# Linear attention into a GELU feed-forward: w_in in two pieces behind the third unit's logits, full-width inter products, seven state buffers, pair results in two stores

## The chip, the cores and the metric

One core of a Trainium2 chip runs the whole kernel. The metric is device microseconds of one execution, and lower is better. The core has TensorE (PE, matmuls; its weight loads are shown as PEld), VectorE (DVE), ScalarE (ACT), GpSimd (POOL) and SyncE (SP, which here only issues transfers). Every engine works through its own list of instructions strictly in order; engines wait for each other through semaphores, and transfers run on 16 DMA engines that all queues share.

## What is computed

Four batches, eight heads, 768 tokens, head size 48. First a gated linear attention with a running state, then a feed-forward block with exact GELU on the 3072 tokens of 384 values:

```python
f = 1.0 / (1.0 + np.exp(-f_logit))
for t in range(S):
    state = f[:, :, t, :, None] * state + np.einsum('bhd,bhe->bhde', k[:, :, t], v[:, :, t])
    y[:, :, t] = np.einsum('bhd,bhde->bhe', q[:, :, t], state)
x = y.transpose(0, 2, 1, 3).reshape(B * S, H * D)      # 3072 x 384
h = x @ w_in                                           # 384 x 2048
g = 0.5 * h * (1.0 + erf(h / sqrt(2)))
out = g @ w_out                                        # 2048 x 384
```

Inputs and output are float32; the matmuls of the kernel run in bf16.

## The kernel before

The tokens are cut into 24 chunks of 128 (six per batch). Two chunks make a *unit* (0 to 11); a unit is also one *group* of the feed-forward. The kernel does not emit instructions where it describes them: `Plan.add` collects operations with an engine, an assumed duration, a priority and their buffers, `Plan.run` places them one after another by earliest start and then priority (jittered by the random seeds in `SEEDS`), and the last loop emits them in that order. So each engine's list is the planner's order, and on the chip nothing overtakes in it. Buffers come from `Slots`; the eight PSUM banks `ps` are split into four for the feed-forward (`s_fh`) and four for attention (`s_m`, also `s_ap`). Where the planner left TensorE idle in the first 30 us, the emitting loop fills in matmuls on a zero tile (`junk`, L947).

Operations are named in the plan; these names, with the unit or chunk number behind them, are used in what follows:

- **E, L** (ACT, L494, L497): exp and log of one minus the gate, on the unit's loaded logits `fl`. **C** (PE, L521 or L526/L527, with the column sums L515/L523): running sums of the logs. **G** (DVE, L535): in the units of `G1D` the second chunk's sums are not multiplied again but are the first's minus one term. **RG, GT, GL** (ACT, L543, L549, L565/L570): exponentials of the sums.
- **KP, QP** (DVE, some POOL, L576): scaled k and q, into `sc`. **VC** (POOL or ACT, L583): v in bf16.
- **Tk, Tq** (PE, L611): transposes of `sc`; **KQ** (DVE or ACT, L617) copies them to `kq`. In units 4 to 11 (`KDMA`) a DMA transpose **KD** (SP, L599) does both.
- **A** (PE, L784 in pair units, L722 in others): scores; **AM** (DVE, L631): masking.
- **S** (PE, L806/L745): k times v of a chunk; **R** (DVE, L651/L655), **T** (POOL, L657) and **SB** (POOL, L662) carry the state from chunk to chunk.
- **YI** (PE, L826) and **YX** (PE, L705): output inside the chunk, and from the carried state; **Y** (L758, L699) is both in units that are no pair. **YB** (L675) evacuates; **XT** (PE, L691) and **X** (L694), or a DMA transpose **XD** (L679), give `xT`.
- **F1.g.u** (PE, L875): six 128x256 matmuls, tile u of group g of x w_in; tiles 0 to 3 need the first 1024 columns of w_in, 4 to 7 the rest. **GE** (ACT, L885): GELU. **F2.n.r** (PE, L896): quarter r of g w_out for chunk n, which needs tiles 2r and 2r+1. **O** (L901) evacuates, **st** (SP, L906) stores.

exp/log and GELU live in different ACT tables: each change costs a table load (L953).

Units 0 to 4 are *pair* units (`PAIRS`): a partition holds two neighbouring tokens, so that one descriptor brings 96 values, and matmuls use half or a quarter of the array (`mode=1` in the plan). GELU puts the tokens of these units back in order by a strided write.

Loads are issued in the order of `LOADS`: f, k, v, q of a unit by SP, pieces of w_in (`i`) and w_out (`o`) by POOL, as instructions in POOL's list (`ii`, `io`). When the issuing queue changes, the transfer waits for an earlier one of the other queue to land (the "gate" in `load`): a POOL load waits for the one four places back, an SP load for one two places back. So `i0` (1024 columns) waits for the landing of f1, and `i1` for that of k2:

```python
LOADS = ['f0', 'k0', 'v0', 'q0', 'f1', 'v1', 'k1', 'q1', 'i0', 'k2', 'f2', 'v2', 'q2', 'i1', 'i2', 'i3', 'o0', 'o1', 'o3', 'o2', 'f3', ...]
```

Of the kernel before, what the change touches and what calls it, by code (L numbers as in the profile page):

```python
# [15 lines left out]

# [7 lines left out]
TURN = 0.1  # L24

SPREAD, SEED = (1.0, 97)

SEEDS = [1643, 41, 3215, 1275, 2533, 2502, 823, 887, 1264, 763, 2447, 3095]

NUDGE = {}  # L30
XA = 0.0
# [48 lines left out]
class Op:  # L80
    __slots__ = ("eng", "dur", "fn", "bufs", "prio", "deps", "table", "start", "end", "vis", "seq", "name",
                 "left", "outs", "inst", "chain", "opens", "lag", "lat", "port", "mode", "held")


class Plan:

# [3 lines left out]
    def add(self, eng, dur, fn, rd=(), wr=(), bufs=(), prio=0.0, deps=(), table=None, name="", chain=None, opens=None, lag=0.0, lat=None, port=False, mode=0, held=False):  # L92
# [5 lines left out]
        o.held = held  # L98
        o.seq = len(self.ops)
# [16 lines left out]
    def run(self):  # L116
        free = dict.fromkeys(list(LAT), 0.7)
        free["DMA"] = 1.8
        rng = random.Random(SEED)
        own = [random.Random(x) for x in SEEDS]  # L120
        for o in self.ops:
            if o.prio > -5:
                k = min(max(int(o.prio % 1000) // 20, 0), len(SEEDS) - 1)
                o.prio += rng.uniform(-SPREAD, SPREAD)
                if SEEDS[k]:
                    w = (0.5, 1.0, 3.0, 8.0)[SEEDS[k] % 4]
                    o.prio += own[k].uniform(-w, w)
            o.prio += NUDGE.get(o.name, 0.0) + (XA if o.table == "exp" and o.prio > 40 else 0.0)
# [10 lines left out]
        while ready:  # L139
# [28 lines left out]
            if o.eng == "PE" and o.mode != mode:  # L168
                mode = o.mode
                d += TURN  # L170
# [29 lines left out]

SIZES = [2, 2, 2, 2, 2, 2, 2, 2, 2, 2, 2, 2]
PAIRS = [0, 1, 2, 3, 4]
WIN = [1024, 512, 512]
EG = [0, 1]
ET = [0, 1]
EX = [0]
EA = [0]
SPLIT = []  # L220
HVC = [1]
HKQ = [0, 2, 6]
HYB = [1, 5]
HX = [4]
GKP, GQP = ([2], [3])
GAM = []
ODVE = [0, 1, 2, 4, 6, 7, 8, 9, 10, 11, 12, 13, 14, 16, 17, 18, 19, 20, 21, 22, 23]
XDMA = [5, 6, 7, 8, 9, 10, 11]
KDMA = [4, 5, 6, 7, 8, 9, 10, 11]
AJ = [2, 3, 4, 5, 6, 7, 8, 10, 11]  # L230
NGT = 4
GLD = []
G1D = [2, 3, 4]
YJ = [2, 3, 4]
ROWS = [16, 17, 18, 19]
AMX = []
WARM = 30.0
LOADS = ['f0', 'k0', 'v0', 'q0', 'f1', 'v1', 'k1', 'q1', 'i0', 'k2', 'f2', 'v2', 'q2', 'i1', 'i2', 'i3', 'o0', 'o1', 'o3', 'o2', 'f3', 'k3', 'q3', 'u4', 'v3']
LOADS += [f"u{n}" for n in range(12) if f"u{n}" not in LOADS and f"c{2 * n}" not in LOADS and f"f{n}" not in LOADS]
# [3 lines left out]
def kernel(  # L243
# [14 lines left out]
    NCH = B * nC  # L258
    d_model = moe_w_in.shape[0]
# [42 lines left out]
    s_rr, s_tn = slots(3, [C, P2, 2 * D], F32, "rr"), slots(3, [C, P2, 2 * D], F32, "tn")  # L302
    s_sb = slots(3, [C, P2, 2 * D], BF16, "sb")
    s_yb = slots(3, [C, 2, HD], BF16, "yb")
    s_os = slots(4, [C, d_model], F32, "osb")
    s_xT = {s: slots({1: 4, 2: 4}.get(s, 2), [C, s, KO, C], BF16, f"xT{s}") for s in set(SIZES)}
    s_gT = {s: slots({1: 4, 2: NGT}.get(s, 2), [C, FO, s * C], BF16, f"gT{s}") for s in set(SIZES)}
# [15 lines left out]

# [30 lines left out]
    for i in range(3):  # L354
        P.add("DVE", 0.2, lambda i=i: nc.vector.memset(
            s_sb.tiles[i].rearrange("p a b -> p (a b)").bitcast(F32), 0.0), wr=[f"sbz{i}"], prio=-70)
# [5 lines left out]
    z_sb = [f"sbz{i}" for i in range(3)]  # L362
# [7 lines left out]
    U = [dict(fl=s_fl.new(), lf=s_lf.new(), pair=u in PAIRS, **{nm: s_in[nm].new() for nm in s_in}) for u in range(NU)]  # L370
# [8 lines left out]

    order, pools = [], []  # L380

    def load(eng, issue, wr, bufs, dur, name):
        i = len(order)
        gate = None
        if i and order[i - 1][0] != eng:
            back = 4 if eng == "pool" else 2
            for j in range(i - back, -1, -1):
                if order[j][0] != eng:
                    gate = order[j][1]
                    break  # L390

# [9 lines left out]
        if prev is not None and order[-1][0] != eng:  # L401
            prev.lat = 2.2
        gd = [gate] if gate is not None else []
        if eng == "pool":
# [15 lines left out]
    def src(a, n):  # L420
        b, c = divmod(n, nC)
        return a[b, :, c * C:(c + 1) * C, :].rearrange("h t d -> t h d")

    def srcp(a, u):
        b, c = divmod(2 * u, nC)
        return a[b, :, c * C:(c + 2) * C, :].rearrange("h (p j) d -> p h (j d)", j=2)

    win_src = moe_w_in.rearrange("(kk p) f -> p kk f", p=C)
    wo_src = moe_w_out.rearrange("(r p j) m -> r p j m", r=4, j=4)
    for what in LOADS:  # L430
        m = int(what[1:])
        if what[0] in "ucfkqv":
# [5 lines left out]
            if x["pair"]:  # L438
                assert what[0] != "c"
                for nm, a in names:  # L440
                    if what[0] not in ("u", nm[0]):
                        continue
                    if nm == "fl" and m in SPLIT:
                        for i in range(2):
                            load("sp", lambda x=x, a=a, m=m, i=i: nc.sync.dma_start(
                                out=x["fl"].t().rearrange("p (h x) -> p h x", h=H)[:, 4 * i:4 * i + 4], in_=srcp(a, m)[:, 4 * i:4 * i + 4]),
                                [("fl", 2 * m + i)], [x[nm]], 0.85, f"fl{m}.{i}")
# [12 lines left out]
        elif what[0] == "i" and m < len(WIN):  # L460
            load("pool", lambda m=m: nc.gpsimd.dma_start(out=win[m], in_=win_src[:, :, wcol[m]:wcol[m] + WIN[m]]),
                 [f"win{m}"], [], {512: 1.97, 1024: 3.95}[WIN[m]] + (0.5 if order[-1][0] == "sp" else 0.0), what)
# [4 lines left out]
    def decays(u):  # L467
# [33 lines left out]
        last = 2 * u + 1 if (2 * u + 1) % nC == nC - 1 else None  # L501
# [84 lines left out]

    St = {}

# [3 lines left out]
    def turn(u, kq):  # L592


        for j in range(2):
# [13 lines left out]
            def trans(i, tpv=tpv, sc=sc):  # L609
# [7 lines left out]
            P.add("ACT" if help_ else "DVE", 0.86 if help_ else 0.61, lambda tpv=tpv, j=j, help_=help_: copier(help_)(  # L617
                kq.t()[:, :, :, j, :].rearrange("a i p t -> a (i p) t"), tpv().rearrange("a i p t -> a (i p) t")),
# [17 lines left out]
    def carry(n, sp, mm, mmdur, mmrd, mmbufs, first_c):  # L636
# [16 lines left out]
        else:  # L653
            old = St["t"]
            P.add("DVE", 0.475, lambda: nc.vector.tensor_tensor(rr.t(), spf(), old.t(), ALU.add),  # L655
                  rd=[("sp", n), ("tn", n - 1)], wr=[("rr", n)], bufs=[sp, rr, old], prio=pr + PRI["S"] - 0.5, name=f"R{n}")
            P.add("POOL", 0.83, lambda: nc.gpsimd.tensor_tensor(tn.t(), rr.t(), glb(), ALU.mult),  # L657
                  rd=[("rr", n), ("gl", n)], wr=[("tn", n)], bufs=[rr, tn, gl], prio=pr + 2, name=f"T{n}")
        St["t"] = tn
# [42 lines left out]
    def interp(yp, kq, cc, osb):  # L702
        for p in range(P2):
            for j in range(2):
# [3 lines left out]
    def attn_nat(u):  # L708
# [3 lines left out]
        for j in range(2):  # L712
# [11 lines left out]
            if u in AJ:  # L724
                both.append((n, amm, aps, ams))
                if j:
                    P.add("PE", 0.46, lambda both=tuple(both): [b[1]() for b in both], mode=1, rd=[("kq", n - 1), ("kq", n)],
# [5 lines left out]
            P.add("PE", 0.23, amm, mode=1, rd=[("kq", n)], wr=[("ap", n)], bufs=[kq] + aps + ams, prio=pr + PRI["A"], opens=aps[0], name=f"A{n}")  # L733
            mask_scores(aps, ams, ("am", n), f"AM{n}", ("ap", n), pr, mask, "mask")
        for j in range(2):
            n = 2 * u + j
            c, x, pr = n % nC, X[n], 10 * n
            sc, vb, ams = x["sc"], x["vb"], amss[j]
            osb = St.get("sb") if c else None
            if c < nC - 1:  # L740
# [6 lines left out]
                St["sb"] = carry(n, sp, smm, 0.175, [("kp", n), ("vb", n)], [sc, vb], c == 0)  # L747
# [4 lines left out]
            def ymm(j=j, ams=ams, vb=vb, yp=yp, osb=osb):  # L752
                if osb is not None:
                    inter(yp, lambda p: kq.t()[:, 1, p, j, :], osb, True)
                for hh in range(2):
# [6 lines left out]
                  rd=[("am", n, 0), ("am", n, 1), ("vb", n), ("kq", n)] + ([("sb", n - 1, 0), ("sb", n - 1, 1)] if c else []),  # L762
# [3 lines left out]
    def attn_pair(u):  # L766
# [6 lines left out]
        sps = [s_m.new(), s_m.new()] if (n0 + 1) % nC < nC - 1 else [s_m.new()]  # L773
        ams, both = [], []
        for jk in range(2):
# [3 lines left out]
            def amm(jk=jk, aps=aps):  # L779
                for p in range(P2):  # L780
                    for cc in range(2):
                        for hh in range(2):
                            r, t = slice(64 * hh, 64 * hh + 64), slice(64 * cc, 64 * cc + 64)
                            nc.tensor.matmul(aps[hh].t()[t, p * C:(p + 1) * C].rearrange("a (j t) -> a j t", j=2),  # L784
# [16 lines left out]
        def smm():  # L801
            for p in range(P2):
# [6 lines left out]
        P.add("PE", 0.45, smm, mode=1, rd=[("kp", n) for n in ns] + [("vb", n) for n in ns],  # L809
              wr=[("sp", n) for n in ns[:len(sps)]], bufs=sps + scs + vbs, prio=pr + PRI["S"], opens=sps[0], name=f"S{u}")  # L810
        osb = St.get("sb") if n0 % nC else None
        for cc in range(len(sps)):
            St["sb"] = carry(ns[cc], sps[cc], None, 0, None, None, ns[cc] % nC == 0)
            if not cc:
                mid = St["sb"]
# [16 lines left out]
        if u in YJ:  # L832
            olds = [(cc, o) for cc, o in enumerate((osb, mid)) if o is not None]

            def joint():
                intra()
                for cc, o in olds:
                    interp(yps[cc], kq, cc, o)
            P.add("PE", 0.5 + 0.2 * len(olds), joint, mode=1,
# [147 lines left out]
```

## Time and profile before

| | |
|---|---|
| Median of 3 runs | 182.56 us (182.15 to 182.91) |
| Span of the profiled execution, first to last instruction | 181.1 us |
| Granted TensorE clock | 1.00 |
| TensorE busy | 171.7 us, 95% of the span |
| ACT, DVE, POOL busy | 125.2, 96.3, 53.6 us |
| First F1 matmul starts | 20.67 us |
| F1 matmuls (576) and F2 matmuls (368 of 384 columns) | 68.7 and 66.0 us busy |
| ACT table loads | 15, of 1.28 us |

The profiled execution's own time is not listed apart from its span; the median of the runs lies 1.5 us above the span, and that is taken for what lies around it (launch, and the end of the last store). "Busy" counts a matmul from its first to its modelled last cycle, so consecutive matmuls overlap: a 128x256 matmul is shown 273 ns long, but the next starts 109 ns after it. A wait is therefore read from the start of one instruction to the start of the next, and not from the busy share alone.

### The profile page before, as it was taken

The numbers are of one execution on the slowest core, as the hardware profiler recorded it, in microseconds if no ns is written. First come the engines' busy times: TensorE is split into PE (matmuls) and PEld (weight loads), VectorE is DVE, ScalarE is ACT, GpSimd is POOL, SyncE is SP. The second block draws the span as 40 slices with busy tenths as digits, with TensorE's granted clock in tenths as the row PEclk, the third lists the DMA queues.
The fourth block names the chain that finished last, engine by engine and source line by source line (L and its number), as shares of the span: only waits on it lengthen the run. The fifth ranks groups of instructions, "written<-read, shape, count | busy, mean of one in ns | idle before, by whom it ended". The sixth has DMA issues, their size and how long they took to land.

```text
span 181.1 us, 4916 instructions
## 1 busy us (share of the span) xinstructions
PE 171.7 (95%) x1990; PEld 132.3 (73%) x1990; DVE 96.3 (53%) x194; ACT 125.2 (69%) x212; POOL 53.6 (30%) x116
## 2 busy tenths in 40 slices
PE   7788889999999999988999999999999999999993
PEld 2356669966787688785779689976697986886972
DVE  5289750058898564244896692527691625362110
ACT  2775198963899189999967759777585578560720
POOL 7657870003043641140176113112435110300000
PEclk9999999999999999999999999999999999999999
DMA  6999999949997898999999999999999872814102
GB/s 148 261 261 226 268 170 203 200 115 267 278 266 142 186 197 170 249 227 171 216 179 213 215 175 207 195 187 189 185 245 181 181 162 47 166 37 91 43 0 87
DMA packets 106998, 32.61 MB, mean 180 GB/s; under 512 B 102113, under 2 KB 106081, under 8 KB 106977
## 3 DMA queue, kind: packets, MB, share of 16 engines
q1 hardware_dynamic: 105056, 29.07, 79.7%
q0 software_dynamic: 1776, 3.15, 9.8%
q8 instruction: 15, 0.25, 0.6%
q10 hardware_dynamic: 144, 0.10, 0.2%
q14 instruction: 7, 0.05, 0.1%
HBM read 25.17 MB, written 4.72 MB: 165 GB/s over the span
## 4 chain that ended last, share of the span: by engine, by line
PE 64%; ACT 15%; DMA 15%; SPq 3%; issue 1%; DVE 0%; DVEq 0%
PE ps L875 26%; PE ps L896 25%; ACT gT L885 7%; DMA fl<-in_f_logit_dram 7%; DMA win<-in_moe_w_in_dram 5%; ACT L953 4%; SPq L449 3%; DMA kq<-sc 2%; PE ps L722 2%; PE ps L758 2%; PE ps L917 1%; ACT gt L549 1%; PE ps L521 1%; PE ps L699 1%; PE ps L745 1%
## 5 line engine op out<-in xcount | busy, mean ns | idle before, releaser
L885 ACT ACTIVATE gT<-ps 128x512 bf16<-128x512 f32 x96 | 57.5, 671 | 24.6 <-PE ps L875 23.0
L875 PE MATMUL ps<-xT,win 128*128 128x256 bf16 x576 | 68.7, 273 | 1.3 <-ACT gT L885 0.9
L896 PE MATMUL ps<-wout,gT 128*128 128x384 bf16 x368 | 66.0, 326 | 0.0
L875 PEld LDWEIGHTS <-win 128*128 128x128 bf16 x576 | 61.6, 114 | 3.9 <-issue 1.2
L896 PEld LDWEIGHTS <-gT 128*128 128x128 bf16 x368 | 34.2, 98 | 19.5
L583 POOL CAST vb<-vt 128x384 bf16<-128x384 f32 x22 | 12.6, 584 | 52.5 <-DMA vt<-in_v_dram 52.4
L631 DVE TENSOR_TENSOR am<-ps,mask 128x512 bf16<-128x512 f32 x28 | 17.6, 684 | 15.1 <-PE ps L722 15.1
L901 DVE COPY osb<-ps 128x384 f32<-128x384 f32 x20 | 11.1, 556 | 25.9 <-PE ps L896 18.2
L657 POOL TENSOR_TENSOR tn<-rr,gl 128x384 f32<-128x384 f32 x16 | 14.0, 872 | 35.2 <-DVE rr L655 34.6
L576 DVE TENSOR_TENSOR sc<-qt,gt 128x384 bf16<-128x384 f32 x23 | 14.0, 616 | 13.7 <-ACT gt L549 13.7
L576 DVE TENSOR_TENSOR sc<-kt,rg 128x384 bf16<-128x384 f32 x23 | 13.5, 597 | 11.3 <-ACT rg L543 11.3
L953 ACT ACT_TABLE_LOAD x15 | 19.2, 1283 | 0.3
L662 POOL CAST sb<-tn 48x192 bf16<-48x192 f32 x40 | 14.8, 371 | 11.6 <-DVE tn L651 6.6
L494 ACT ACTIVATE fl<-fl 128x768 f32<-128x768 f32 x12 | 10.1, 842 | 10.5 <-DMA fl<-in_f_logit_dram 10.5
L675 DVE CAST yb<-ps 128x384 bf16<-128x384 f32 x22 | 11.9, 555 | 7.4 <-PE ps L758 3.7
L631 DVE TENSOR_TENSOR am<-ps,maskp 128x512 bf16<-128x512 f32 x20 | 12.5, 684 | 2.2 <-PE ps L784 1.4
L543 ACT ACTIVATE rg<-ps 128x384 f32<-128x384 f32 x21 | 10.3, 503 | 4.4 <-PE ps L523 2.8
L549 ACT ACTIVATE gt<-ps 128x384 f32<-128x384 f32 x21 | 10.2, 503 | 3.9 <-PE ps L523 3.3
L947 PE MATMUL ps<-junk 128*128 128x512 bf16 (+3 forms) x36 | 10.4, 423 | 2.1 <-POOL junk L939 1.3
L655 DVE TENSOR_TENSOR rr<-ps,tn 128x384 f32<-128x384 f32 x16 | 8.9, 553 | 3.5 <-POOL tn L657 1.8
L497 ACT ACTIVATE lf<-fl 128x768 bf16<-128x768 f32 x12 | 10.1, 843 | 0.4
L947 PEld LDWEIGHTS <-junk 128*128 128x128 bf16 x36 | 3.6, 111 | 6.2 <-issue 3.5
(74 smaller groups left out, 130.4 us busy)
## 6 DMA issues: line engine op xcount, KB each, us to landing
out_dram<-osb SPq DMA_DIRECT2D x19, 192.0 KB, 3.1
fl<-in_f_logit_dram SPq DMA_DIRECT2D x14, 192.0 KB, 3.8
kt<-in_k_dram SPq DMA_DIRECT2D x14, 192.0 KB, 3.8
qt<-in_q_dram SPq DMA_DIRECT2D x14, 192.0 KB, 3.7
vt<-in_v_dram SPq DMA_DIRECT2D x14, 192.0 KB, 3.9
fl<-in_f_logit_dram SPq DMA_DIRECT2D x5, 384.0 KB, 6.2
kt<-in_k_dram SPq DMA_DIRECT2D x5, 384.0 KB, 6.2
vt<-in_v_dram SPq DMA_DIRECT2D x5, 384.0 KB, 5.7
```

What stands on the lines that cost most here:

```text
L549: P.add("ACT", 0.40, lambda g=gps[j], gtv=gtv: nc.scalar.activation(gtv(), g.t()[:, 0:HD].rearrange("q (p h d) -> q p h d", h=2, d=D), AF. ...
L576: P.add("POOL" if pl else "DVE", 0.80 if pl else 0.475, lambda a=a, y=y, j=j, w=w, pl=pl, b=(gtv if w else rg): (nc.gpsimd if pl else nc.v ...
L583: P.add("ACT" if hv else "POOL", 0.40 if hv else 0.47, lambda y=y, j=j, hv=hv: (nc.scalar.copy if hv else nc.gpsimd.tensor_copy)(y["vb"].t ...
L631: P.add("POOL" if pl else "DVE", 1.15 if pl else 0.61, lambda hh=hh, pl=pl: (nc.gpsimd if pl else nc.vector).tensor_tensor(ams[hh].t(), ap ...
L657: P.add("POOL", 0.83, lambda: nc.gpsimd.tensor_tensor(tn.t(), rr.t(), glb(), ALU.mult), rd=[("rr", n), ("gl", n)], wr=[("tn", n)], bufs=[r ...
L662: P.add("POOL", 0.36, lambda hh=hh: nc.gpsimd.tensor_copy(sb.t()[64 * hh:64 * hh + D, :, D * hh:D * hh + D], tn.t()[64 * hh:64 * hh + D, : ...
L675: P.add("ACT" if help_ else "DVE", 0.40 if help_ else 0.475, lambda: copier(help_)(yb.t()[:, i, :], yp.t()[:, 0:HD]), rd=[("yp", n)], wr=[ ...
L875: nc.tensor.matmul(hps.t()[:, i * tok:(i + 1) * tok].rearrange("a (s t) -> a s t", s=s), col(fo)[:, kk, :], xT.t()[:, :, kk, :], start=(kk ...
L885: nc.scalar.activation(to, fr, AF.Gelu)
L896: nc.tensor.matmul(op.t()[:, 0:d_model], gT.t()[:, fo, s_ * C:(s_ + 1) * C], wout[fo // 4][:, fo % 4, :], start=(fo == 0), stop=(fo == FO ...
L947: nc.tensor.matmul(o.opens.t()[:, 0:w], junk[:, 0:C], junk[:, 0:w], start=True, stop=True, skip_group_check=True)
L953: nc.scalar.preload_act_table_set({"exp": "natural_log_exp_and_others", "gelu": "gelu_and_others"}[o.table])
```

## The change

- **Loads.** w_in comes in two pieces of 1024 columns. `i0` is now the tenth load, behind f2 (unit 2's logits); within units 0 to 4 the order of k, q, v is changed. The gates are found by adding up the assumed durations of the loads between instead of counting places; worked out, `i0` still waits for f1, `i1` now waits for f2 (it was k2), f3 for `o0` (it was `o3`), k3 for `o3`.
- **Order.** The random priorities are replaced by a list, one number per operation. Every engine's order changes.
- **Pair units.** In units 0 to 3, `kq` is laid out so that one 128-wide product replaces two 64-wide ones in YX (L705); scores read 128 columns in one piece.
- **State.** `tn` and `sb` have seven buffers instead of three.
- **Results of units 0 to 4.** GELU keeps the pair order, and each of their chunks is stored by two transfers of 64 rows.
- **Lists.** `G1D` and `YJ` shrink from [2, 3, 4] to [3], `AJ` loses unit 3; who does KQ, VC, YB, X and O is redistributed; planner durations and turn costs change.

Code for a third kind of unit (`HALVES`, `DENSE`) comes with the diff but its lists are empty and it emits nothing.

```diff
-PAIRS = [0, 1, 2, 3, 4]
-WIN = [1024, 512, 512]
+WIN = [1024, 1024]
+NTN, NSB = 7, 7
+RST = [0, 1, 2, 3, 4]
...
-AJ = [2, 3, 4, 5, 6, 7, 8, 10, 11]
+AJ = [2, 4, 5, 6, 7, 8, 10, 11]
-G1D = [2, 3, 4]
-YJ = [2, 3, 4]
+G1D = [3]
+YJ = [3]
+AHEAD = 5.5
-LOADS = ['f0', 'k0', 'v0', 'q0', 'f1', 'v1', 'k1', 'q1', 'i0', 'k2', 'f2', 'v2', 'q2', 'i1', 'i2', 'i3', 'o0', 'o1', 'o3', 'o2', 'f3', 'k3', 'q3', 'u4', 'v3']
+LOADS = ['f0', 'v0', 'k0', 'q0', 'f1', 'q1', 'k1', 'v1', 'f2', 'i0', 'q2', 'k2', 'v2', 'i1', 'o2', 'o0', 'o3', 'f3', 'o1', 'k3', 'q3', 'f4', 'q4', 'v4', 'k4', 'v3', 'u5', ...]
...
+        if PRIO:
+            for o, p in zip(self.ops, PRIO):
+                o.prio = p / 20
...
-        if i and order[i - 1][0] != eng:
-            back = 4 if eng == "pool" else 2
-            for j in range(i - back, -1, -1):
-                if order[j][0] != eng:
+        if i and eng != "act" and order[i - 1][0] != eng:
+            ahead = 0.0
+            for j in range(i - 1, -1, -1):
+                if order[j][0] != eng and ahead >= (AHEAD if eng == "pool" else 1.4):
                     gate = order[j][1]
                     break
+                ahead += order[j][1].dur
...
+            def evac(tpv=tpv, j=j, help_=help_):
+                if U[u]["pair"]:
+                    copier(help_)(kq.t().rearrange("a i p c (j r) -> a (i p) c j r", j=2)[:, :, :, j, :],
+                                  tpv().rearrange("a i p (c r) -> a (i p) c r", c=2))
+                    return
...
-    def interp(yp, kq, cc, osb):
+    def interp(yp, kq, cc, osb, full):
         for p in range(P2):
+            if full:
+                nc.tensor.matmul(yp.t()[:, 96 * p:96 * p + 96], kq.t()[:, 1, p, cc, :], osb.t()[:, p, :], start=False, stop=False, skip_group_check=True)
+                continue
             for j in range(2):
...
+    def perm(n):
+        return U[n // 2]["pair"] or U[n // 2]["hs"]
...
-                if U[ns[0] // 2]["pair"]:
+                if perm(ns[0]) and ns[0] // 2 not in RST:
                     to = to.rearrange("p (n t j) -> p n j t", j=2, t=64)
...
             def store(n=n, osb=osb):
+                if perm(n) and n // 2 in RST:
+                    for j in range(2):
+                        nc.sync.dma_start(out=out[rc[n] * C:(rc[n] + 1) * C, :].rearrange("(r j) m -> j r m", j=2)[j], in_=osb.t()[64 * j:64 * j + 64, :])
+                    return
```

In the order as built, the lists around the first feed-forward tiles read as follows (unit and chunk numbers behind the names, F1 and GE with group and tile):

```
PE before:  ... A1.1 A1.0 F1.0.1 F1.0.3 F1.0.2 YI1 YX2 YX3 F1.0.0 XT2 XT3 C4 F1.1.3 ...
PE after:   ... A1.1 C4 C5 A1.0 F1.0.1 F1.0.2 F1.0.0 YI1 Tq4 YX2 YX3 Tk4 Tq5 Tk5 F1.0.3 XT2 XT3 A2 S2 F1.1.3 ...
ACT before: ... YB1 KQ2 E2 L2 GE0.1 GE0.3 GE0.0 GE0.2 ...
ACT after:  ... VC2 VC3 YB0 YB1 E2 X0 L2 RG4 GT4 RG5 GT5 GL5 GE0.1 GE0.2 GE0.0 KQ4 GE0.3 X3 GE1.3 ...
DVE after:  ... KQ3 X1 AM1.1 AM1.1 R3 AM1.0 AM1.0 QP5 QP4 KP4 KP5 YB2 YB3 KQ5 X2 AM2.0 AM2.1 R4 ...
POOL before: ... T2 SB2 SB2 T3 SB3 SB3 ii1 ii2 io0 VC4 VC5 io1 io3 io2 T4 ...
POOL after:  ... KP2 QP3 ii1 io2 io0 T2 SB2 SB2 T3 SB3 SB3 VC5 VC4 T4 io3 SB4 SB4 io1 ...
```

## The prediction

> **What bounds the kernel.** First the page's busy shares and its chain of work that ended last, then busy time in five stretches, then the chain in order of time, last the matmul rows around each wait.
>
> ```profile
> PE 171.7 (95%) x1990; PEld 132.3 (73%) x1990; DVE 96.3 (53%) x194; ACT 125.2 (69%) x212; POOL 53.6 (30%) x116
> ...
> PE 64%; ACT 15%; DMA 15%; SPq 3%; issue 1%; DVE 0%; DVEq 0%
> ```
>
> TensorE sets the end; no other engine is near full. The stretches (columns: stretch, its length, busy us of PE, PEld, DVE, ACT, POOL with instruction counts, clock, DMA share, GB/s) show where TensorE is not full:
>
> ```profile
> 0.00:20.67 20.67, 16.50 (x229) 8.89 (x230) 14.23 (x42) 11.17 (x20) 14.61 (x44) 1.00 1.09 230
> 20.67:27.35 6.68, 5.88 (x93) 4.73 (x94) 3.30 (x7) 4.73 (x7) 5.21 (x10) 1.00 1.12 198
> 27.35:85.00 57.65, 56.26 (x710) 44.39 (x709) 29.28 (x56) 47.07 (x77) 13.56 (x26) 1.00 1.00 205
> 85.00:178.06 93.06, 93.06 (x962) 74.33 (x960) 49.10 (x90) 62.18 (x111) 20.22 (x37) 1.00 0.81 156
> ```
>
> From 85 us to the last matmul at 178.06 there is no gap; then 3.04 us of tail. Between 27.35 and 85 TensorE loses 57.65 - 56.26 = 1.4 us, plus the modelled drain (273 - 109 = 0.16 us) that each of some four waits hides: 2.1 us. Before 27.35 the DMA engines are full (share above 1), and the chain says what is waited for:
>
> ```profile
> 4.38 6.17 DMA fl<-in_f_logit_dram
> 10.55 0.30 issue
> 10.84 9.78 DMA win<-in_moe_w_in_dram
> 20.63 0.05 issue
> 20.67 2.16 PE ps L875 x18
> ```
>
> So the end is: the moment from which TensorE is full, plus its remaining work, plus its few later waits. I take as marker the start of F1.1 (group 1's first tile): 27.35 us before.
>
> **The start, step by step.** The built order puts C4 and C5 ahead of F1.0, and E2, X0, L2 and unit 2's exponentials ahead of the first GELU. All hang on f2, now SP's ninth load. Before, the ninth was k2:
>
> ```profile
> 10.32 1.39 SPq L449 DMA_DIRECT2D kt<-in_k_dram  x1
> ...
> 10.84 0.94 POOL L461 DMA_DIRECT2D win<-in_moe_w_in_dram  x1 [1.96 <-DMA fl<-in_f_logit_dram]
> ...
> 22.56 0.84 ACT L494 ACTIVATE fl<-fl 128x768 f32<-128x768 f32 x1 [3.89 <-DMA fl<-in_f_logit_dram]
> ```
>
> ```profile
> kt<-in_k_dram SPq DMA_DIRECT2D x1, 384.0 KB, 10.7
> ```
>
> k2 was issued at 10.32 and took 10.7 us, beside `i0`, which POOL issued at 10.84 on f1's landing; the eighth load had taken 6.2. `i0` still waits for f1, so f2 takes k2's place: it lands at 21.0, `i0` at 20.6, q2 at 22.5. f2 gains 1.5 us, but F1.0, which started at 20.67, now stands behind it:
>
> - ACT: E2 21.1, X0 22.0, L2 22.4 to 23.25 (0.87 for E by the rows 22.56 and 23.43, 0.4 for X).
> - C4 on PE at 23.3. RG follows C's first matmul by 0.5 us (6.33 to 6.85): RG4 23.8, GT4 24.2 to 24.7, RG5, GT5, GL5 until 25.5 (0.38 apart, rows 37.60, 37.99, 38.36). Table load 1.28: first GELU at 26.8 (25.59 before).
> - A1.0 uses C4's bank, freed by GT4: 24.75. F1.0.1, .2, .0 follow, 25.1 to 27.1 (six times 0.109 each).
> - DVE: masks 0.46 after A1.0 starts (18.74 to 19.20): 25.2, two of 0.62; then QP5, QP4, KP4, KP5 0.48 apart (rows 38.12 to 39.54), YB2, YB3 0.5 each, KQ5 0.68: done at 30.1. PE keeps pace (YI1 27.1, transposes until 29.0).
> - A2 0.67 (42.50 to 43.17 before), S2 0.54, turns: F1.1 starts at 31.5.
>
> The marker moves by 31.5 - 27.35 = 4.15 us. In exchange unit 2's transposes (16 x 0.056 = 0.9), A2 (0.67) and S2 (0.54) are done by then: 2.1 us. Net loss 2.05 us.
>
> POOL's queue: `ii1` now stands ahead of T2 and waits for f2. It sat behind SB3 before and was issued at 21.33, so its data come no later. But T2, which ran at 17.70, waits with it and runs after the issue of `ii1`, `io2`, `io0` (0.81 + 0.77 + 0.58 by the rows) at 23.2; R3 behind it on DVE ends near 24.8, ahead of the masks at 25.2. Free by 0.4 us; beyond that it pays one for one.
>
> **After the marker.**
>
> - C9 on PE instead of DVE (`G1D`): 2 x 0.162 = +0.32. C5 is in the start already.
> - A3 in two halves: one more change of array layout, +0.09 and +0.14 by the gaps around 62.6 and 63.2, less the 0.07 inside: +0.18.
> - Full-width YX: sixteen half matmuls took 0.34 us (47.54 to 47.88), eight of 128x96 at 0.042 take 0.34. Nothing is saved but a layout change of 0.1 in each of units 2 and 3: -0.2.
> - Plain GELU in units 0 to 4: medians 784 ns (28.5 to 36 us) against 597 (100 to 120 us), so 0.58 against 0.48 start to start, some 4 us of ACT. The built order has 17 table loads for 15, which gives 2.6 back. ACT had 57.65 - 47.07 = 10.6 us idle in the third stretch: 0, both ways.
> - Seven `tn`/`sb` buffers: no wait of T or SB on a buffer is among the longest waits, their idle time ends on R: 0. Four more clearing writes on DVE, 4 x 0.22, lie in its 4.6 us wait before 7.75: 0.
> - Ten more store issues on SP, 0.58 each, 5.8 us over 45: they delay loads behind them. Cover: f5's second half is the next load needed. Its two transposes ahead wait for KP9 at 57.6; 1.3 us each and one store put it at 59.8, landing 4.3 later at 64.1, E5 and L5 to 65.8, group 3's first GELU at 70.9. PE has work up to F1.3.7 at 71.7 without it. Slack 0.8 us; past it the price is one for one.
> - f3 is issued on `o0`'s landing (32.6) instead of 37.75, lands at 36.8, wanted at 47.6: 0, and it takes away ACT's wait of 2.58 us before 41.94.
>
> **The later waits.** The 2.1 us sit at these rows:
>
> ```profile
> 55.05 1.15 PE L875 MATMUL ps<-xT,win 128*128 128x256 bf16 x9 [0.44 <-ACT gT L885]
> ...
> 79.20 2.78 PE L875 MATMUL ps<-xT,win 128*128 128x256 bf16 x24 [0.45 <-ACT gT L885]
> ...
> 84.14 0.40 PE L722 MATMUL ps<-kq 64*128 64x128 bf16 x8 [0.37 <-DMA kq<-sc]
> ```
>
> Two are logit tiles that wait for a GELU during an exponential batch, one is A11 waiting for its transposes. Walking the new lists with the same durations, PE meets its inputs with 0.1 to 1 us to spare: C6 needs L3 at 49.3 and comes at 49.5, A11 comes at 84 when its transposes landed near 77, F2.8.0 finds its GELU at 84.5. I take the 2.1 us as gained and 0.5 us as new small waits (bounds 0 and 2.1).
>
> **Sum.** +2.05 + 0.32 + 0.18 - 0.2 - 2.1 + 0.5 = +0.75. The span of 181.1 becomes 181.9, and with the same 1.46 us around it 183.3, against the median of 182.56. A measurement tells about 0.5% (0.9 us: 181.65 to 183.47) from no change, so this is no change that could be told, on the slow side. With the unknowns at their ends (later waits 0 to 2.1, start +-0.7): 182.3 to 185.0.
>
> **A rule against the change.** In the new order TensorE has nothing from A1.1 and its filler at 19.9 to C4 at 23.3, 3.4 us; the widest such hole before, once started, was 0.9 us. What a pause does shows at the start:
>
> ```profile
> 1.31 4.59 PE L947 MATMUL ps<-junk 128*128 128x512 bf16 x12 [1.31 <-POOL junk L939]
> ...
> 17.68 0.92 PE L947 MATMUL ps<-junk 128*128 128x512 bf16 x4
> ```
>
> 0.38 us each on average from rest, 0.23 when running. The Trainium skill ("TensorE: Matmul & The Clock Gate", Part 1: The HAM clock gate) says that the array's clock falls to half after about 3.4 us of idle and comes back after as long a busy time. By it the hole is just at the limit; the sum would be the rival below. No row here shows a pause of that length.
>
> **Rivals.**
>
> - *Cold restart, slower.* The hole sends TensorE back to the pace of its first rows, about half. The work from 23.3 on, C4 and C5 0.85, A1.0 0.3, three F1 1.96, takes twice as long; YI1 stands behind F1.0.0, so the marker moves by 2.3 of these 3.1 us: 185.6. Against it: only just long enough. It decides if the first matmuls after the hole are twice as far apart as 0.109 us.
> - *f2 passes i0, faster.* SP issues f2 0.5 us before POOL issues `i0`; served in order of issue, f2 lands 1.5 us after the eighth load, at 16.6. Then E2 starts at 17.3, GT4 ends at 20.8, `i0` lands at 22.1, F1.0 ends at 24.1, q2's products start at 22.7, F1.1 at 28.2: net -1.25 instead of +2.05, 180.0. Against it: k2 in the same place was not served first.
> - *The later waits stay.* The walk is optimistic; from f5 landing 0.8 us late each us counts, as does each GELU late for a bank: +2 over the sum, 185.2. For it: 2.1 us were lost before in the same places.
>
> **Chances.** Forecast 0.47 (0.26 of it within 0.5%, 0.18 above, 0.03 below), f2 first 0.25, cold restart 0.14, later waits 0.14. Faster 0.28, same 0.26, slower 0.46. The range reaches from just above the one rival to the others: 179.9 to 185.8; of the forecast alone 182.3 to 185.0.
>
> **What would show it.** E2 waiting for `fl` until 21 and the first F1 matmul (L1172 of the changed kernel) at 25 and not 20.7; F1.1 at 31.5; POOL idle until 21 before its second load of w_in (L532); masks and products on DVE without a gap from 25.2; TensorE then full, with under 0.6 us of waits to 85. Wrong would be: E2 by 18, matmul pace of 0.22 us at 25, or gaps at the exponential batches around 47 to 57 and 61 to 71.

## The result and the profile after

The changed kernel takes 188.76 us (median of four: 187.08, 188.65, 188.88, 190.40) against 182.43 before on the same chip: 1.032 times, interval 1.027 to 1.037. The forecast was 183.3 with a range up to 185.8. The mean granted clock of the four is 1.000, 0.991, 0.982 and 0.982 in that order; the profiled one is the longest (190.40), span 188.6 us. Ratios, here and below, leave out executions over 1.5% above the fastest of their kernel (here the longest); medians take in all.

The page of the changed kernel (span; busy us of each engine; TensorE's busy tenths and granted clock in 40 slices of 4.7 us; the chain that ended last):

```profile
span 188.6 us, 4884 instructions
...
PE 174.1 (92%) x1963; PEld 133.1 (71%) x1966; DVE 96.0 (51%) x190; ACT 129.0 (68%) x221; POOL 50.1 (27%) x114
...
PE   7886499999999999979929999999999999999992
...
PEclk9999979999999999999987999999999999999999
...
PE 79%; DMA 10%; SPq 7%; ACT 1%; issue 1%; DVE 1%; DVEq 0%
```

TensorE's busy time hardly grew; its row has a hole in slice 5, where the prediction had put one, and two in slices 18 and 21 that it had not seen. The clock falls behind the first and the last (slices 6, 21 and 22). The stretches of the changed kernel, cut at the first F1, at F1.1 and behind the second hole (columns as in the prediction):

```profile
0.00:25.13 25.13, 18.51 (x236) 10.03 (x239) 15.44 (x44) 14.44 (x29) 15.74 (x46) 0.96 1.11 232
25.13:31.61 6.48, 6.48 (x130) 5.63 (x127) 6.15 (x11) 4.88 (x7) 1.80 (x5) 0.91 1.05 198
31.61:102.50 70.89, 66.43 (x787) 51.46 (x786) 38.38 (x71) 52.34 (x90) 17.01 (x34) 0.98 1.02 188
102.50:185.22 82.72, 82.72 (x819) 66.03 (x816) 35.62 (x65) 57.31 (x96) 15.57 (x31) 1.00 0.72 145
```

F1.1, the marker, starts at 31.61 (27.35 before): 4.26 us later. From the marker to the last matmul it is 185.22 - 31.61 = 153.6 us against 178.06 - 27.35 = 150.7: 2.9 more, where the prediction had expected some 3.4 less. The tail grew by 0.36. Together 7.5, the difference of the spans; this execution is 1.6 us over the median. So 2.9 + 3.4 = 6.3 us were lost behind the marker. TensorE's rows there (start, length, line, operation, and idle time with what ended it):

```profile
78.76 2.11 PE L1193 MATMUL ps<-wout,gT 128*128 128x384 bf16 x12
81.96 0.34 PE L1025 MATMUL ps<-vb,sc 128*128 128x96 bf16 x4 [1.08 <-DVE sc L647]
```

```profile
94.01 0.81 PE L1193 MATMUL ps<-wout,gT 128*128 128x384 bf16 x4
98.19 1.44 PE L1172 MATMUL ps<-xT,win 128*128 128x256 bf16 x6 [3.37 <-DMA xT<-yb]
99.42 0.52 PE L1025 MATMUL ps<-vb,sc 128*128 128x96 bf16 x4
```

Start to start, 1.25 and 3.5 us are lost. The first stall is S12 waiting for KP12; on VectorE QP13 stands ahead of KP12, and it waited for the load of q:

```profile
80.88 0.56 DVE L647 TENSOR_TENSOR sc<-qt,gt 128x384 bf16<-128x384 f32 x1 [1.73 <-DMA qt<-in_q_dram]
```

The second is F1.5.4 waiting for XD11, the transposition of chunks 10 and 11. Both transfers are SP's. SP's own row of the changed kernel shows what stands ahead of them (L871 is KD, L1203 the stores, L956 XD):

```profile
70.33 3.36 SPq L871 DMA_TRANSPOSE kq<-sc  x2
73.74 2.67 SPq L1203 DMA_DIRECT2D out_dram<-osb  x4
76.45 0.59 SPq L528 DMA_DIRECT2D kt<-in_k_dram  x1
77.09 0.68 SPq L528 DMA_DIRECT2D qt<-in_q_dram  x1
...
82.74 4.20 SPq L871 DMA_TRANSPOSE kq<-sc  x2
86.98 0.59 SPq L528 DMA_DIRECT2D fl<-in_f_logit_dram  x1
88.09 2.51 SPq L1203 DMA_DIRECT2D out_dram<-osb  x4
90.65 0.59 SPq L528 DMA_DIRECT2D kt<-in_k_dram  x1
91.28 0.69 SPq L528 DMA_DIRECT2D qt<-in_q_dram  x1
92.01 0.58 SPq L528 DMA_DIRECT2D vt<-in_v_dram  x1
92.69 1.91 SPq L956 DMA_TRANSPOSE xT<-yb  x1
```

Each store of a chunk is now two issues, so two chunks hold SP for 2.5 to 2.7 us. XD11's data were there at about 89.1; it was issued at 92.69 and landed at 98.14. In the kernel before it had been issued at 88.87 and landed at 92.20, and a store of a chunk was one issue (SP's rows of that kernel):

```profile
81.17 1.45 SPq L906 DMA_DIRECT2D out_dram<-osb  x1
...
88.87 1.23 SPq L679 DMA_TRANSPOSE xT<-yb  x1
```

Behind the second hole the matmuls run at half pace (stretches of 1 us of the changed kernel; the third last column is the clock):

```profile
97.00:98.00 1.00, 0.00 (x0) 0.00 (x0) 0.00 (x0) 0.00 (x0) 0.00 (x0) 0.99 0.92 169
98.00:99.00 1.00, 0.81 (x5) 0.56 (x5) 0.00 (x0) 0.00 (x0) 0.00 (x0) 0.50 1.35 214
```

Twelve F1 matmuls 0.213 us apart instead of 0.109 cost 1.25 us. With 1.25 + 3.5 + 1.25 = 6.0 of the 6.3 us the later loss is accounted for.

### The profile page after: what moved, and what is told of

The parts are those of the page before. It is cut to its first block, busy times and chain, and to the rows that moved or that the text cites. A ratio compares the mean times of both kernels' runs of the same rounds, so it can differ in the third digit from the quotient of the medians.

```text
span 188.6 us, 4884 instructions
## 1 busy us (share of the span) xinstructions
PE 174.1 (92%) x1963; PEld 133.1 (71%) x1966; DVE 96.0 (51%) x190; ACT 129.0 (68%) x221; POOL 50.1 (27%) x114
## 4 chain that ended last, share of the span: by engine, by line
PE 79%; DMA 10%; SPq 7%; ACT 1%; issue 1%; DVE 1%; DVEq 0%
PE ps L1172 34%; PE ps L1193 30%; DMA fl<-in_f_logit_dram 5%; SPq L520 5%; DMA xT<-yb 3%; PE ps L1002 2%; DMA qt<-in_q_dram 2%; PE ps L1218 1%; SPq L1203 1%; PE ps L1025 1%; PE ps L1038 1%; PE ps L883 1%; PE ps L976 1%; PE ps L1065 1%; PE ps L592 1%
## 5 line engine op out<-in xcount | busy, mean ns | idle before, releaser
L1182 ACT ACTIVATE gT<-ps 128x512 bf16<-128x512 f32 x96 | 56.2, 598 | 27.8 <-PE ps L1172 24.5
L1172 PE MATMUL ps<-xT,win 128*128 128x256 bf16 x576 | 71.1, 277 | 3.4 <-DMA xT<-yb 3.4
L654 POOL CAST vb<-vt 128x384 bf16<-128x384 f32 x20 | 10.5, 534 | 68.9 <-DMA vt<-in_v_dram 68.9
L1198 DVE COPY osb<-ps 128x384 f32<-128x384 f32 x18 | 10.0, 556 | 20.3 <-PE ps L1193 11.4
L939 POOL CAST sb<-tn 48x192 bf16<-48x192 f32 x40 | 13.9, 349 | 9.4 <-DVE tn L928 7.5
L647 DVE TENSOR_TENSOR sc<-kt,rg 128x384 bf16<-128x384 f32 x23 | 14.2, 638 | 4.3 <-ACT rg L614 4.2
L952 DVE CAST yb<-ps 128x384 bf16<-128x384 f32 x21 | 10.9, 553 | 7.9 <-PE ps L1038 3.7
L620 ACT ACTIVATE gt<-ps 128x384 f32<-128x384 f32 x23 | 11.1, 501 | 2.4 <-PE ps L592 1.1
L1248 PE MATMUL ps<-junk 128*128 128x512 bf16 (+3 forms) x29 | 9.1, 447 | 1.5 <-POOL junk L1240 1.3
L883 PE MATMUL ps<-ident,sc 128*128 128x128 bf16 x64 | 5.6, 220 | 1.5 <-DVE sc L647 1.4
```

The costliest lines, as they stand in the source:

```text
L620: P.add("ACT", 0.40, lambda g=gps[j], gtv=gtv: nc.scalar.activation(gtv(), g.t()[:, 0:HD].rearrange("q (p h d) -> q p h d", h=2, d=D), AF. ...
L647: P.add("POOL" if pl else "DVE", 0.80 if pl else 0.475, lambda a=a, y=y, j=j, w=w, pl=pl, b=(gtv if w else rg): (nc.gpsimd if pl else nc.v ...
L654: P.add("ACT" if hv else "POOL", 0.40 if hv else 0.47, lambda y=y, j=j, hv=hv: (nc.scalar.copy if hv else nc.gpsimd.tensor_copy)(y["vb"].t ...
L939: P.add("POOL", 0.36, lambda hh=hh: nc.gpsimd.tensor_copy(sb.t()[64 * hh:64 * hh + D, :, D * hh:D * hh + D], tn.t()[64 * hh:64 * hh + D, : ...
L952: P.add("ACT" if help_ else "DVE", 0.40 if help_ else 0.475, lambda: copier(help_)(yb.t()[:, i, :], yp.t()[:, 0:HD]), rd=[("yp", n)], wr=[ ...
L1172: nc.tensor.matmul(hps.t()[:, i * tok:(i + 1) * tok].rearrange("a (s t) -> a s t", s=s), col(fo)[:, kk, :], xT.t()[:, :, kk, :], start=(kk ...
```

## The experiments

Each edit is made to the changed kernel without planning it anew, so that every engine keeps its order except where the diff says otherwise. "Moved" means: taken out of the emitted order and put behind the operation named. Kernels with the same time in the third column ran on one chip, which is that of the kernel before there; the ratio is to it.

| kernel | median us | before there | ratio, interval |
|---|---|---|---|
| whole stores | 184.50 | 183.01 | 1.0073 (1.0025 to 1.0121) |
| XD11 first | 194.94 | 183.01 | 1.0665 (1.0607 to 1.0723) |
| warm at F1.5 | 190.69 | 183.01 | 1.0428 (1.0366 to 1.0490) |
| w_in later | 196.49 | 183.01 | 1.0737 (1.0674 to 1.0799) |
| changed kernel again | 190.19 | 182.14 | 1.0361 (1.0287 to 1.0435) |
| rows by GELU | 184.53 | 182.14 | 1.0134 (1.0095 to 1.0172) |
| second half on ACT | 185.67 | 182.14 | 1.0219 (1.0156 to 1.0282) |
| F1 in the hole | 184.33 | 182.14 | 1.0135 (1.0113 to 1.0156) |
| A1 early | 184.98 | 182.21 | 1.0146 (1.0119 to 1.0173) |
| before, with halves | 185.76 | 182.21 | 1.0212 (1.0159 to 1.0266) |
| A1 early, no filler | 183.72 | 182.73 | 1.0057 (1.0027 to 1.0087) |
| logits first | 181.63 | 182.73 | 0.9956 (0.9925 to 0.9988) |

**Whole stores.** Ten chunks stored in one transfer each, their rows left in the pair order (so the output isn't the reference's):

```diff
-                if perm(n) and n // 2 in RST:
+                if False:
                     for j in range(2):
```

> The changed kernel with its order, but each chunk of the pair units stored in one transfer of 128 rows, as the other chunks are (the rows of these ten chunks then stand in the order of the pair units, which is not the reference's). Theory A, SP's order and length: the half stores are only a part of what stands ahead of the transposition of units 10/11 on SP (2.5 us for four of them against some 1.2 for two whole ones); it is issued 1.2 to 1.5 us earlier, the stall in front of F1.5.4 falls from 3.5 to about 2.1, the one of 1.25 us at 80.55 to 0.3 or less: time 186.4 (185.6 to 187.2). Theory B, the half stores alone are the cause: both stalls go and the clock stays up at 98 us: time 183.5 or less. Theory C, stores don't matter: 188 or more.

184.50. The stall at 80 us is gone, and the one ahead of F1.5.4 is down to 0.64 us, the largest wait left behind the marker. Theory B in its place, 1.0 us over its time. (The profiled execution is a longer one, 186.61, with the marker at 33.42.) My own theory A, that half stores were a third of it, falls.

**XD11 first.** Moved: `XD11` behind YB10, `st6` behind XD11.

> The changed kernel with one transfer in another place of SP's order: the transposition of chunks 10/11 stands ahead of st6, st7 and the three loads kt7.1, qt7.1, vt7.1 instead of behind them. Theory A: it is issued at 89 to 89.5 us as soon as its data are there, lands by 94.5, F1.5.4 stalls 0.5 us or less, the granted clock stays full from 94 to 101: 3.5 and 1.2 us come back, time 184.0 (183.2 to 185.0). Rival, the transposition is slow by itself (5.46 us from issue to landing against 3.3 in the kernel before): it lands at 95.5 or later, the stall is 1.5 us or more and the time 186.5 or more. Rival, the loads that are passed become late in turn: a new stall of over 1 us behind a load of unit 7 after 95 us, time 185 to 187.

194.94, worse by far. XD11 was issued at 91.74 and took 2.75 us to land, so it is not slow by itself, but the loads it passed came late in turn. TensorE's and VectorE's rows of this kernel:

```profile
97.24 0.82 PE L1172 MATMUL ps<-xT,win 128*128 128x256 bf16 x6
102.23 0.48 PE L1025 MATMUL ps<-vb,sc 128*128 128x96 bf16 x4 [4.17 <-POOL vb L654]
```

```profile
100.32 0.56 DVE L647 TENSOR_TENSOR sc<-kt,rg 128x384 bf16<-128x384 f32 x1 [3.45 <-DMA kt<-in_k_dram]
```

`kt` of unit 7, passed by XD11, landed at 100.22 instead of 93.49. SP had stood from 89.9 to 91.74 waiting for XD11's data, so everything behind XD11 was issued later: `kt` 62.4 us after the marker instead of 59.0. S15 waited 4.3 us for its v, the clock fell again. The second rival's mechanism holds, in this order the transfers behind XD11 have not the slack to let it pass; its time of 185 to 187 was far too low. Its marker (33.15) and the stall at 80 us (2.3 us) came out worse too, so not all of the 194.94 is the reordering's.

**Warm at F1.5.** Fourteen matmuls on a zero tile ahead of F1.5.4.

```diff
+            for i in range({'F1.5.4': 14}.get(o.name, 0)):
+                nc.tensor.matmul(o.opens.t(), junk[:, 0:C], junk, start=True, stop=True, skip_group_check=True)
```

> The changed kernel with 14 matmuls on data that nobody reads put into TensorE's stall in front of F1.5.4. Theory A: the stall stays, but the 128x256 matmuls behind it run at 0.11 us instead of 0.21, the granted clock is full in the slices from 98 to 101 us: 1.2 us less in the runs in which the clock fell there, so 187.4 (186.8 to 188.0), and less spread between runs. Rival, the slow matmuls behind the stall are held by something other than the clock (their data, the weights): pace unchanged, time 188.4 or more.

In this kernel's rows the two F1 groups behind the filler run at full pace:

```profile
98.20 2.97 PE L1251 MATMUL ps<-junk 128*128 128x512 bf16 x13
101.00 0.82 PE L1172 MATMUL ps<-xT,win 128*128 128x256 bf16 x6
```

0.82 us for six, against 1.44 in the changed kernel: the slow pace was the clock. The time of 190.69 misses the 187.4 and shows no gain (ratio 1.043, the changed kernel's are 1.032 and 1.036). It doesn't tell the price either, as the changed kernel did not run on that chip, and in this kernel the first stall was 3.0 us and the slow stretch at the start 16 matmuls long.

**w_in later.** Moved: `ii0` behind SB1.

> The changed kernel with the first w_in piece issued 3.4 us later, behind the state copies of the first unit on POOL, so that the third unit's logits pass it. Theory A, the start is lost because the logits share the queues with w_in and everything up to the first GELU stands behind their gates: logits land at 16.5 to 17.5, the first gate matmul is at 19 to 20, the first F1 at about 25 at full pace with no hole of 2 us ahead of it, F1.1 starts at 28.5 to 29.5, time 186.4 (185.4 to 187.4). Rival, w_in's landing alone sets the start: F1.1 stays at 31.2 or later and the time at 188 or more.

196.49, a miss that taught something: the gate matmuls came earlier, but `ii1`, which waits for the logits, was now issued at 16.95 (20.87 in the changed kernel), and the w_in and w_out pieces behind it starved `kt2` and `vt2`, which landed at 31.9 and 33.0. TensorE waited 5.7 us for KP5 at 26.9. The start theory was not tested by it.

**The changed kernel again**, as control on the next chip.

> The changed kernel itself, for comparison on the same chip: 187 to 190.5, with the stalls at 80 to 82 us and 94 to 98 us.

190.19 (187.53 to 192.20), profiled at 190.53: a hole of 2.7 us at 20 us, stalls of 1.8 and 3.2 us at the same places.

**Rows by GELU.** The pair rows are put in order by the GELU's write, as before the change, and each chunk is stored whole.

```diff
-                if perm(ns[0]) and ns[0] // 2 not in RST:
+                if perm(ns[0]):
                     to = to.rearrange("p (n t j) -> p n j t", j=2, t=64)
...
-                if perm(n) and n // 2 in RST:
+                if False:
```

> The changed kernel in its own order, the row order of the pair units made as in the kernel before: the GELU writes its tile in token order and each chunk goes out in one store of 128 rows. Theory B, the second store of each pair chunk on SP is the cause of the later stalls: as with whole stores, no stall over 0.7 us between 40 us and the end, 184.5 (183.8 to 185.3), and the GELU's strided write costs nothing. Rival, the strided write makes the GELU longer and TensorE waits for it: 185.5 or more.

184.53, against 190.19 on the same chip: by the medians the second stores cost 5.7 us, by the ratios (1.0361 and 1.0134 of 182.14) 4.1. From the marker to the last matmul it is 147.5 us, against 153.6 and 153.4 in the two profiles of the changed kernel. The GELU's strided write (60.0 us in all instead of 56.2) costs nothing that TensorE sees. No wait over 0.7 us is left behind the marker. SP's row of this kernel:

```profile
73.22 1.13 SPq L1207 DMA_DIRECT2D out_dram<-osb  x2
...
86.14 1.02 SPq L1207 DMA_DIRECT2D out_dram<-osb  x2
...
90.00 1.77 SPq L956 DMA_TRANSPOSE xT<-yb  x1
```

Counted from the marker, XD11 is issued at 58.1 us instead of 61.1 and lands at 61.8 instead of 66.5.

**Second half on ACT.**

```diff
-                        nc.sync.dma_start(out=out[...
+                        (nc.scalar if j else nc.sync).dma_start(out=out[...
```

> The changed kernel with the second half of each pair store issued on ScalarE's queue instead of SP's: the same transfers, ten fewer issues on SP. Theory B1, what counts is SP's time (0.6 us an issue): both later stalls fall to under 0.7 us, time 184.8 (184.0 to 186.0, the upper part if ScalarE's own issues delay a GELU). Theory B2, what counts is the traffic of half stores, not their issue: the stalls stay as in the changed kernel and so does its time.

185.67: the same transfers, and 4.5 of the 5.7 us are back (by the ratios 2.6 of 4.1). No wait over 0.5 us is left behind the marker, XD11 lands 62.1 us after it, and it is 148.5 us to the last matmul. So it is mostly the issuing queue's time that counts (B1), not the traffic; some 1 us stays. The Trainium skill ("Perfetto Trace Analysis", DMA Optimizations) says that where descriptor generation is the bottleneck, an engine looking busy with it rather than with the transfers, balancing DMAs over the engines that can issue them may help; this pair of runs agrees.

**Only unit 3, and all but unit 3, in halves** (`RST` in both places replaced by a list of units).

> The changed kernel with the rows of units 0, 1, 2 and 4 ordered by the GELU and stored whole; only st6 and st7 go out in halves. Theory B: no stall at 80 us; ahead of F1.5.4 one of 1.0 to 2.0 us stays. If the stalls come from a backlog that the stores of all units build up: none there either, as with all stores whole.

> The changed kernel with the rows of unit 3 alone ordered by the GELU, so that st6 and st7 are stored whole and the other pair units' chunks in halves. Theory B: the stall at 80 us stays (1.2 to 2.0 us) and the one ahead of F1.5.4 falls from 3.5 to between 1.0 and 2.3 us. If st6 and st7 alone made the second stall, it is under 0.6 us.

One execution each, 186.71 and 187.94 (182.21 before there). Halves for st6 and st7 alone: no stall over 0.9 us behind the marker, XD11 lands 61.9 us after it, and from the marker to the last matmul it is 148.3 us (147.5 with all whole, 153.6 with all in halves). Halves for the others: the stall at 80 us stays at 1.25, that ahead of F1.5.4 is gone, one of 1.1 us appears at 116; 150.6 us. The stall at 80 us went as theory B had it: it belongs to the stores of the other units. On the stall ahead of F1.5.4 I was wrong in both: neither set of halves makes it alone, both together do. Alone the two sets cost 0.8 and 3.1 us, together 6.1. This fits lateness that adds up in SP's queue, of which TensorE sees only what exceeds the slack of the transfer behind.

**The kernel before, with halves.**

```diff
-                w = C // 2 if n in ROWS else C
+                w = C // 2 if n in ROWS or n < 10 else C
```

> The kernel before, with the stores of the first ten chunks in two halves of 64 rows, as the changed kernel issues them, and nothing else. Theory B: SP's queue has no room for ten more issues of 0.6 us between 60 and 100 us in that order either, TensorE waits 1.5 us or more in sum, time 184.0 to 187.0. Rival F, the order before had the room that my prediction read from it (half stores cost under 0.5 us there), and only the new order has none: 182.0 to 183.0.

185.76 against 182.21: 3.55 us. The order before had no room for all of them either; rival F falls. The lateness comes out at another transposition (this kernel's rows; 1.35 us more than the usual distance):

```profile
106.17 0.81 PE L896 MATMUL ps<-wout,gT 128*128 128x384 bf16 x4
108.17 1.03 PE L875 MATMUL ps<-xT,win 128*128 128x256 bf16 x8 [1.19 <-DMA xT<-yb]
```

This execution's span is 2.5 us longer than before's (183.6 against 181.1); beside the 1.35 there is a tail longer by 0.7, and the rest lies in smaller waits.

**F1 in the hole.** On the kernel with the rows by GELU. Moved: E2 behind X0; F1.0.1, F1.0.2 behind A1.1.

> The kernel with the rows ordered by the GELU, and at the start two of the F1 groups of the first unit (F1.0.1, F1.0.2) put ahead of the third unit's gate matmuls on TensorE, with their input copy X0 ahead of E2 on ScalarE. Theory D, the start loses 2 us by idle time ahead of C4 and up to 1.4 us more by the clock that falls in it: F1 starts at 21.2, C4 at 22.5 to 23, F1.1 at about 30 us at full clock, time 1.3 to 2.5 us under the kernel with the rows ordered by the GELU. Rival, the marker is set by what follows C4 (masks, KQ5): F1.1 stays at 31 or later and the gain is under 0.7 us.

184.33, the marker at 31.90 (31.89 without): the rival holds. The granted clock was 1.000 throughout, so the 3.4 us at half clock at the start (23.4 to 26.9 in the kernel without the move) had cost little or nothing. It is no clean price: the emitting loop's filler, which goes by planned starts, stood ahead of F1.0.1 (which started at 22.2, not 21.2), and C4 came at 23.52 instead of 22.87; from C4 to A1.0 it then took 1.27 us instead of 1.70. What sets the marker comes behind the gate matmuls.

**A1 early.** Moved, on the same base: A1.0 and its masks behind AM1.1, then F1.0.1, C5, C4, and the exponentials of chunk 5 ahead of those of chunk 4; E2 behind X0.

> The kernel with the rows ordered by the GELU, and at the start A1.0 put ahead of the third unit's gate matmuls instead of behind them (both use one PSUM bank, which A1.0 otherwise gets only when GT4 has read it), then F1.0.1 and the gate matmuls; the exponentials of chunk 5 ahead of those of chunk 4, E2 behind X0. Theory E, the start is set by the chain logits, gate matmul, GT4, bank, A1.0, masks and not by the idle time that F1 could fill: A1.0 starts at 21.5 instead of 24.6, F1.1 at 29.5 to 30.5 instead of 31.9, time 1.2 to 2.2 us under the kernel with the rows ordered by the GELU, 182.3 to 183.3. Rival, the chain through QP5 and KQ5 sets the marker: F1.1 stays at 31.3 or later and the time within 0.6 us of that kernel.

184.98, marker 32.69. The filler again: nine zero matmuls stood ahead of A1.0, which started at 23.31. The theory was not tested, so it was run again without the filler, and with the three F1 groups between the gate matmuls:

> As the kernel with A1.0 early, but without the program's filler matmuls, which it places by planned starts and which in that kernel stood in front of A1.0 for 2 us: on TensorE F1.0.1, A1.0, F1.0.2, the gate matmuls of chunk 5, F1.0.0, those of chunk 4. Theory E, the chain logits, gate matmul, GT4, bank, A1.0, masks sets the start: A1.0 at 21.5 to 22.3, F1.1 at 29.5 to 30.5, time 182.4 to 183.4. Rival, the chain through GT, QP5 and KQ5 sets it: F1.1 at 31.3 or later, 184 or more.

183.72, marker 31.13, A1.0 at 21.45. Three us earlier for A1.0 bring 0.8 at the marker: the bank is a small part. The result lies between the two, nearer to the rival.

**Logits first.** On the kernel with the rows by GELU. Moved: `ii0` behind SB1; `ii1`, `io2`, `io0` behind T3; YI1, YX2, YX3, F1.0.1, F1.0.2 behind AM1.0; five zero matmuls ahead of YI1, no other filler there.

> The kernel with the rows ordered by the GELU, and at the start the third unit's logits alone ahead of w_in: the first w_in piece issued behind the state copies of the first unit, the second piece and the two w_out pieces that follow behind T3, so that they don't starve kt2 and vt2 as they did when the first piece alone was moved; YI1, YX2 and YX3 ahead of F1. Theory G, the landing of the logits at 20.6 to 21 us sets the start: logits at 17, gate matmuls at 19, F1 from 23.3 (w_in's landing), F1.1 at 26.5 to 28.5, time 180.0 to 182.5. Rival, w_in, kt2 and vt2 share the queues and one of them lands after 26 us in the place of the logits: F1.1 at 30 or later, 183.5 or more.

181.63, 0.9956 times the kernel before (0.9925 to 0.9988): the one version that beats both, by 0.4%. E2 starts at 16.6 and F1.1 at 29.28, 2.6 us earlier than without. ScalarE's and TensorE's rows of this kernel:

```profile
16.63 0.90 ACT L565 ACTIVATE fl<-fl 128x768 f32<-128x768 f32 x1
```

```profile
20.25 0.33 PE L597 MATMUL ps<-lf,trip 128*128 128x384 bf16 x1
...
24.26 2.13 PE L1172 MATMUL ps<-xT,win 128*128 128x256 bf16 x18
...
29.28 2.92 PE L1172 MATMUL ps<-xT,win 128*128 128x256 bf16 x25
```

`kt2` and `vt2` landed at 24.2 and 25.5, as in the changed kernel. The marker lies 0.8 us past the expected 28.5 (F1 began at 24.26, not 23.3: YI1 waits for masks), the time within its 180.0 to 182.5. Theory G is borne out in sum: with the logits 4 us earlier the start is 2.6 us earlier. The edit moves other things with them (T2 and R3 ahead of `ii1`, YI1 and YX ahead of F1), and their shares are not separated.

## Why the prediction was wrong, point by point

- **The bound.** Right: from 102.5 us to the last matmul TensorE has no gap, and each us lost ahead of that shows in the end.
- **The start, step by step.** Right. Predicted and measured: E2 21.1 and 20.59, C4 23.3 and 22.60, A1.0 24.75 and 24.55, first F1 25.1 and 25.13, first GELU 26.8 and 26.56, F1.1 31.5 and 31.61. T2 came at 22.80 and R3 ended at 24.24, ahead of the masks: free, as said. That F1.1 came within 0.11 us is in part luck: C4 was 0.7 us early, and from C4 to the first F1 it took 2.53 us, at half clock, where 1.8 had been predicted. The rows of the changed kernel:

```profile
22.60 0.32 PE L597 MATMUL ps<-lf,trip 128*128 128x384 bf16 x1 [2.11 <-ACT lf L568]
...
25.13 2.70 PE L1172 MATMUL ps<-xT,win 128*128 128x256 bf16 x18
...
31.61 0.63 PE L1172 MATMUL ps<-xT,win 128*128 128x256 bf16 x4
```

- **After the marker, and the later waits.** Right in sum where the stores are whole: 179.39 - 31.89 = 147.5 us from the marker on against 150.7, 3.2 less; the prediction's terms (2.1 brought forward, 2.1 of waits gained, 0.5 new, 0.32 + 0.18 - 0.2) give 3.4 less. The terms under 0.4 were not measured one by one. The plain GELU was worth nothing that shows, as said (148.4 us from the marker with it, in the profile of whole stores).
- **"Ten more store issues on SP ... 0": the step that failed.** I had their size (0.58 us each) and the rule (past the slack, one for one), but looked for one load that could be late, f5, and ended the walk at 85 us. The runs put 5.7 us (4.1 by the ratios) in its place in this order and 3.55 in the order before. SP works through its list in order. In the 28 us from 69.6 on its waits add up to 7.3 us; in the same stretch behind the marker they are 11.6 with the rows by GELU. The added issues use up such waits, and past them delay all that follows, up to the transfer with the least slack: XD11, 3.6 us behind its data, landing at 98, past the end of the walk. Nor did the 0.5 us for new small waits cover it.
- **The rule on the clock.** The hole came, 2.1 us long instead of 3.4, and the clock was 0.50 behind it, from 22.9 to 26.3 us. The price of that rival, 2.3 us, was wrong: from E2 to the marker it is 11.02 us, and 10.88 at full clock (F1 in the hole), since the marker hung on the chain behind the logits. Where the half clock lasted 6.8 us, in the profiles of whole stores, XD11 first, warm at F1.5 and only unit 3, the same distance is 1.1 to 1.4 us longer. What did cost 1.25 us was the same mechanism 73 us later, behind a hole the walk hadn't reached.
- **f2 passes `i0`.** It did not: both landed within 0.6 us (20.57, 21.16). Made to happen by hand, with the other moves of that edit, it is worth 2.9 us (184.53 to 181.63, on two chips), near the 3.3 that the rival differed from the forecast by.
- **The later waits stay.** They went; those that came were others.
- **The range.** 182.3 to 185.0 is not the sum with the unknowns at their ends: that gives 183.3 - 0.5 - 0.7 = 182.1 and 183.3 + 1.6 + 0.7 = 185.6.

The forecast's 183.3 is 1.2 us under what the change takes with whole stores (184.5); the miss beyond that is one term of the sum, set at nothing, and the clock behind the stall that it makes.

## What to carry to other kernels

A queue that only issues is an engine with a busy time: add up its issues over the whole stretch until it is idle again, and look for the transfer with the least slack in that stretch, not for the next one. A split of a transfer is free only where what follows on its queue has slack for one more issue; with the second half on another queue most of the price went, here all but some 1 us. And moving one transfer forward on a queue without such slack moves the lateness; removing issues removes it.

## What the runs showed that was not expected

- The clock falls after shorter pauses than the one that I had weighed, and the length of a pause does not decide it. TensorE was idle for 2.1 us ahead of C4, and the clock fell; idle for 2.1 us in XD11 first (to 84.5) and for 2.8 us in warm at F1.5 (to 85.3) it stayed at 1.000. In all 16 traces the changes of the clock lie whole multiples of 3.41 us apart. Cut at these points, the stretch around the first pause and the next one (changed kernel), and the two that the pause of 2.8 us falls into (warm at F1.5):

```profile
19.49:22.90 3.41, 1.21 (x20) 0.66 (x21) 1.60 (x4) 1.95 (x3) 2.03 (x4) 1.00 1.16 278
22.90:26.31 3.41, 3.41 (x36) 1.95 (x34) 1.63 (x3) 3.05 (x6) 3.09 (x7) 0.50 1.15 225
```

```profile
80.20:83.61 3.41, 2.26 (x15) 1.22 (x13) 0.53 (x1) 3.10 (x7) 0.00 (x0) 1.00 0.84 171
83.61:87.02 3.41, 1.74 (x17) 1.20 (x18) 2.72 (x5) 0.70 (x2) 1.00 (x3) 1.00 1.05 206
```

  At full clock, each of the 13 such stretches in which TensorE was busy for less than 45% was followed by one at 0.50; none with more than 58% was, and between these (six stretches from 51% to 58%) both occur. So what counts is how much of one stretch is idle, and a pause that a boundary divides can pass. The Trainium skill ("TensorE: Matmul & The Clock Gate", Part 1) gives a free-running window of 3413 ns, and the slow clock after an idle one; the length agrees, but most stretches that brought the clock down were not idle (35% busy in the rows above).
- The clock stays low for one such period or for two: 3.41 us in the changed kernel, 6.83 (22.15 to 28.98) with whole stores. Each period at half clock takes 0.009 off the mean clock, which fits none, one, two and two of them in the four executions of the changed kernel (1.000, 0.991, 0.982, 0.982). This may be part of why equal programs spread by 3 us here.
- XD11 took 5.46 and 5.2 us from issue to landing in the two profiles of the changed kernel, 2.75 to 3.9 in the others where it can be read. Some 1.8 of the 4.7 us by which it lands later than with the rows by GELU are this; what lengthened it stays open.
